# Query-major score tiles by TensorE transposes in one of eight half-steps of an attention backward pass

## The chip, the cores and the metric

The kernel runs on one core of a Trainium2 chip. The metric is the time of one execution on the device in microseconds (us). The engines are TensorE (PE; its weight loads are shown as PEld), VectorE (DVE), ScalarE (ACT), GpSimd (POOL) and SyncE (SP), which issues most of the transfers; 16 DMA engines carry them.

## What is computed

Forward and gradients of a gated sum of an attention block and a state-space convolution, sequence 2048, width 576, 32 heads of 18. The change touches only the attention:

```python
scores = jnp.einsum("bhqd,bhkd->bhqk", q, k) * (Dh ** -0.5)
p = _softmax(scores, axis=-1)
o = jnp.einsum("bhqk,bhkd->bhqd", p, v)
...
_out, _vjp = jax.vjp(_f, A_x, A_wqkv, A_wo, B_A_re, B_A_im, B_B_re, B_B_im, B_C_re, B_C_im, B_log_dt, B_Dskip, gate_w)
```

The backward pass needs the unnormalised probabilities `exp(score)` in both orientations: key-major (keys on the partitions, queries along the free axis) for the output and for the score gradient, and query-major (queries on the partitions) for the gradient of V. One is the transpose of the other.

## The kernel before

Projections come first, then the attention, then the state-space part and the last products. The attention's order on all engines is written out by hand: instructions stand on each engine in the order in which the loop issues them.

The 32 heads go in 8 groups of four, each head on 32 partitions, and the queries in 4 blocks of 512. One pair of group and block is a unit; there are 32 units. A unit takes 32 half-steps, so that the loop over `G` (L998) runs through 1024 of them, and some more at the end. A half-step does two things side by side, for two different units: the forward side for half-step `G`, and the backward side for `G2 = G - OFF`, with `OFF = 39`.

In each half-step PE issues, in this order:

- P1 (L1020-1022): two matmuls of 32 contraction rows for two heads, key-major scores of 128 keys by 512 queries, into a pair of PSUM banks (`s_pair`, tag `S`, two such pairs in rotation). ACT turns them into `PT` by one exponential of 128x1024 (L1095). There are 41 `PT` tiles in rotation, one made in each half-step.
- a burst of work that goes by slot, where slot is `(G2 + 1) % 8`: the two halves of the gradients of V (slots 0 and 1), Q (2 and 3) and K (5 and 6), or transposes that VectorE copies out (4 and 7). What a burst leaves in PSUM is evacuated by VectorE in slots 1, 3, 4, 6 and 7, but not in slots 0, 2 and 5.
- P3 (L1062-1064): two matmuls for two heads, query-major scores, into the next `S` pair. ACT turns them into `eb` by an exponential of 128x1024 (L1100). The V gradient reads `eb` in slots 0 and 1.
- P2 (L1069-1070): two matmuls for the other two heads, one PSUM bank each (tag `dP`, two banks in rotation). VectorE multiplies each by a half of `PT` into `ds` (L1105).
- accO (L1081): in slots 1, 2, 5 and 6 four more matmuls, the forward output.

The `ds` tiles are transposed by DMA (L1113), and the K gradient reads the result, `dsT`, in slots 5 and 6.

After PE's list is issued, VectorE gets first the evacuation of the burst, and then the multiplications of this half-step. ACT has two exponentials in a half-step: `PT`, then `eb`. Every eight half-steps repeat; below they are called a period. There are 128 of them.

In the profile P1 is the row `ps_P<-QaT_g,KaT_g`, P3 the row `ps_P<-KaT_g,QaT_g`, P2 the row `ps_P<-dOaT,VaT_g`, and all have the helper's line L30. Transposes of a `ds` tile are the row `turn_p` (L843), and their copy is L848.

Of the kernel before, what the change touches and what calls it, by code (L numbers as in the profile page):

```python
# [10 lines left out]
ACT = mybir.ActivationFunctionType  # L11
BF = mybir.dt.bfloat16
# [5 lines left out]
P = 128  # L18


def build(tc, aps, dbg_aps=None, stages=("s1", "attn", "post", "s4", "final")):
    nc = tc.nc
# [6 lines left out]
    def mm(out, lhsT, rhs, start=True, stop=True, **kw):  # L29
        return nc.tensor.matmul(out, lhsT=lhsT, rhs=rhs, start=start, stop=stop, **kw)  # L30
# [31 lines left out]
    with ExitStack() as gctx:  # L62
# [3 lines left out]
        ident_bf = const.tile([P, P], BF, name="ident_bf")  # L66
# [49 lines left out]
        with ExitStack() as ctx:  # L116
# [37 lines left out]
            rows = [QKV_d[ROW0[k_]:ROW0[k_] + H * WID[k_], :].rearrange("(h w) s -> h w s", w=WID[k_]) for k_ in "QKV"]  # L154
# [50 lines left out]
            for m, (h0, hn) in enumerate(hts):  # L205
                fn = hn * DH
                for which in (1, 0, 2):
# [3 lines left out]
                    for tb in range(NBK):  # L211
                        ps = psA.tile([P, TB, P], F32, tag="proj", bufs=4, name="ps_proj")
# [485 lines left out]
        if "attn" in stages:  # L698
            KB = 512
            NQ = S // KB  # L700
            TPQ = KB // P
            DA = HP
            NFILL = {"V": 1, "Q": 0, "K": 0}
            with ExitStack() as ctx:
# [9 lines left out]
                def pt_tile():  # L714

                    x = (ptn[0] - (PTN - 41)) % 41
                    ptn[0] += 1
                    return pts["a" if x < 17 else "bcd"[(x - 17) // 8]][1].tile([P, 2, KB], BF, tag="PT", name="PT")

                PTN = NG * NQ * NT * 2  # L720
                apsp = ctx.enter_context(tc.tile_pool(name="aps", reuse_waits="tile", bufs=1, space=bass.MemoryType.PSUM))
# [105 lines left out]
                def row(ps, l, r, j):  # L827
                    r0 = HP * j
                    mm(ps, lhsT=l[r0:r0 + DA], rhs=r[r0:r0 + DA], tile_position=(r0, 0))

                def s_pair(kind):
                    return apsp.tile([P, 2, KB], F32, tag="S", bufs=2, name="ps_" + kind)

                def by_pe(p):

                    return {NPF: 0, NPF + 1: 1}.get(p, 2)
# [161 lines left out]
                for G in range(NTOT + OFF + 24):  # L998
# [4 lines left out]
                    if G < NTOT:  # L1003
                        u, s = divmod(G, NST)
                        g, b = units[u]
# [7 lines left out]
                    if 0 <= G2 < NTOT:  # L1013
                        u2, s2 = divmod(G2, NST)
                        r2 = (units[u2][0], units[u2][1], s2)
                    rows = []
                    if r1:
                        g, b, i, j0 = r1
                        T = grp_t[g]
                        ps = s_pair("P1")  # L1020
# [12 lines left out]
                    elif 0 <= m_ < NTOT // 8:  # L1033
                        u_, kq = divmod(m_, NQ)
                        g, b = units[u_]
# [12 lines left out]
                        else:  # L1048
                            p = 2 * kq + (slot == 4)
# [5 lines left out]
                    if r2:  # L1055
                        g, b, s2 = r2
                        T = grp_t[g]
                        U = UN[(g, b)]
                        par_ = (s2 + OFF) % 2
                        jo = 2 * par_  # L1060
                        kq, ii = s2 // 8, (s2 % 8) // 2
                        ps = s_pair("P3")  # L1062
                        for x in range(2):
                            row(ps[:, x, :], T["QaT", b][:, ii * P:(ii + 1) * P], T["KaT", kq], jo + x)
                        rows.append(("P3", g, b, (kq, ii), jo, ps))
                        i2 = s2 // 2
                        for x in range(2):
                            j2 = 2 * (1 - par_) + x
                            ps = apsp.tile([P, KB], F32, tag="dP", bufs=2, name="ps_P2")  # L1069
                            row(ps, T["VaT", i2 // TPQ][:, (i2 % TPQ) * P:(i2 % TPQ + 1) * P], U["dOaT"].rearrange("p t q -> p (t q)"), j2)  # L1070
                            rows.append(("P2", g, b, i2, j2, ps))
                    tail = []
                    if G % 8 in (0, 3, 4, 7) and G >= 3:
                        i_ = (G - 3) // 8 * 4 + {3: 0, 4: 1, 7: 2, 0: 3}[G % 8]
                        u_, i_ = divmod(i_, NT)
                        if 0 <= u_ < NU:
                            g, b = units[u_]
# [13 lines left out]
                    for (kind, g, b, i, j, ps) in rows:  # L1091
                        U = UN[(g, b)]
                        if kind == "P1":
                            U["PT"][i, j // 2] = pt_tile()
                            nc.scalar.activation(U["PT"][i, j // 2], ps, ACT.Exp)  # L1095
                        elif kind == "P3":
                            e = work.tile([P, 2, KB], BF, tag="eb", bufs=8, name="eb")
                            for x in range(2):
                                U["eb"][(i[0], i[1], j + x)] = e[:, x, :]
                            nc.scalar.activation(e, ps, ACT.Exp)  # L1100
                        else:
                            if i not in U["ds"]:
                                U["ds"][i] = work.tile([P, 4, KB], BF, tag="ds", bufs=5, name="ds")
                                U["dsn", i] = 0
                            nc.vector.tensor_tensor(U["ds"][i][:, j, :], ps, U["PT"][i, j // 2][:, j % 2, :], op=A.mult)  # L1105
                            U["dsn", i] += 1
                            nj = 3 if by_pe(i // 2) >= 2 - i % 2 else 4
                            if U["dsn", i] == nj:
                                p = i // 2
                                assert j == nj - 1  # L1110
                                if i % 2 == 0:
                                    U["dsT", p] = work.tile([P, 2, 4 * TPQ, P], BF, tag="dsT", bufs=3, name="dsT")
                                nc.sync.dma_start_transpose(out=U["dsT", p][:, i % 2, 0:nj * TPQ, :],  # L1113
                                                            in_=U["ds"][i][:, 0:nj, :].rearrange("p j q -> p (j q)"))
# [125 lines left out]
        if "final" in stages and "s4" in stages:  # L1240
# [14 lines left out]
            with ExitStack() as ctx:  # L1255
# [18 lines left out]
                with ExitStack() as actx:  # L1274
# [10 lines left out]
                    for q, r_ in enumerate((0, 4, 12)):  # L1285
                        n_ = 2 if r_ == 12 else 1
# [89 lines left out]
                    row = pf.tile([1, D], F32, name="dlrow")  # L1376
# [19 lines left out]
                for t in range(NT):  # L1396
# [15 lines left out]
                    ps = pps.tile([P, 2, 512], F32, tag="ps2b", name="ps_a")  # L1412
# [12 lines left out]
                    ps = pps.tile([P, 2, 512], F32, tag="ps2b", name="ps_dx")  # L1425
# [17 lines left out]
                for c, (f0, fsz) in enumerate(dch):  # L1443
                    ob = work.tile([P, D], BF, tag="dwo_bf", bufs=3, name="dwo_bf")
                    for u, (e0, esz) in enumerate(HALF):
                        ps = pps.tile([P, 512], F32, tag="one", name="ps_dwo")
# [14 lines left out]
def kernel(  # L1461
    tc,
    A_x, A_wqkv, A_wo, B_u, B_A_re, B_A_im, B_B_re, B_B_im, B_C_re, B_C_im, B_log_dt, B_Dskip, gate_w, grad_out,
    out_0, out_1, out_2, out_3, out_4, out_5, out_6, out_7, out_8, out_9, out_10, out_11, out_12,
):
    aps = dict(A_x=A_x, A_wqkv=A_wqkv, A_wo=A_wo, B_u=B_u, B_A_re=B_A_re, B_A_im=B_A_im, B_B_re=B_B_re, B_B_im=B_B_im,
               B_C_re=B_C_re, B_C_im=B_C_im, B_log_dt=B_log_dt, B_Dskip=B_Dskip, gate_w=gate_w, grad_out=grad_out,
               out_0=out_0, out_1=out_1, out_2=out_2, out_3=out_3, out_4=out_4, out_5=out_5, out_6=out_6, out_7=out_7,
               out_8=out_8, out_9=out_9, out_10=out_10, out_11=out_11, out_12=out_12)
    build(tc, aps)  # L1470
# [30 lines left out]
```

The softmax here doesn't subtract the row's maximum and nothing guards it: scores larger than these inputs give would overflow.

## Time and profile before

| | us |
|---|---|
| timed runs | 2879.93 (median), 2881.84, 2875.08 |
| span of the profiled execution | 2881.9 |
| first `PT` exponential to the last `eb` exponential | 205.1 to 2180.0 |
| ACT busy in the whole span | 2374.4 |
| DVE busy in the whole span | 2361.3 |
| PE busy in the whole span | 2469.8 |

No time beside the span is recorded for the profiled execution itself; its span lies 2.0 us above the median of the timed runs. "Busy" is the union of an engine's instructions, where PE's are pipelined and their ends modelled. In the page's groups and in the timeline a row gives the start or the time in sum, the mean of one instruction, its engine, line and operation, its output and inputs, their shapes and, with x, how many there are. Neighbouring instructions overlap, so that the distance between two starts is shorter than what one of them takes.

### The profile page before, as it was taken

To read this page: it belongs to the slowest core of one execution; us is meant where nothing else is said; L and a number is where in the kernel's file an instruction comes from. 1 tells how busy PE (TensorE), PEld (TensorE's weight loads), DVE (VectorE), ACT (ScalarE), POOL (GpSimd) and SP (SyncE) were. 2 spreads that over 40 slices of the span, in tenths; PEclk is the share of its full clock that TensorE was granted. 3 is DMA by queue.
4 is the path that set the end of the run, shared out by engine and by line. 5 is a ranking of instruction groups with operands and counts; after the bars stand their busy time and mean duration, and the time that the engine had idled before them with its cause. 6 is when DMAs were issued, how large, how long until landed. Compare 5 with 4: busy or idle time off the path is not lost.

```text
span 2881.9 us, 69539 instructions
## 1 busy us (share of the span) xinstructions
PE 2469.8 (86%) x27132; PEld 1188.0 (41%) x27132; DVE 2361.3 (82%) x4143; ACT 2374.4 (82%) x2792; POOL 1609.6 (56%) x2657
## 2 busy tenths in 40 slices
PE   4778898898888889888999989898986889888699
PEld 2332333333233233233333323333324788788467
DVE  4444999898898899889999989999975899999854
ACT  2449999999899999999999999999964777877121
POOL 1037888887788888888878878888511000000010
PEclk7876999999899999999999999999966888888799
DMA  8864889999999999998998998899798888885895
GB/s 223 162 169 87 154 160 174 159 161 161 162 160 159 175 161 159 167 166 152 168 174 153 163 168 159 156 172 165 139 163 206 238 220 219 232 212 156 249 227 131
DMA packets 1293343, 499.99 MB, mean 173 GB/s; under 512 B 1187774, under 2 KB 1263136, under 8 KB 1283796
## 3 DMA queue, kind: packets, MB, share of 16 engines
q1 hardware_dynamic: 1260388, 434.38, 78.6%
q0 software_dynamic: 20624, 53.26, 7.6%
q10 hardware_dynamic: 12000, 7.90, 1.0%
q8 instruction: 212, 3.47, 0.5%
q14 instruction: 119, 0.97, 0.1%
HBM read 144.48 MB, written 99.69 MB: 85 GB/s over the span
## 4 chain that ended last, share of the span: by engine, by line
ACT 35%; PE 25%; DVE 24%; DMA 7%; issue 6%; SPq 2%; POOL 0%; ACTq 0%; DVEq 0%; POOLq 0%
ACT eb L1100 21%; ACT PT L1095 13%; PE ps_P L30 7%; DVE ds L1105 7%; DVE tz L559 3%; DMA dsT<-ds 3%; PE accV L30 2%; DVE HG L563 2%; DVE tz L562 2%; PE turn_p L843 2%; PE ps_dx L30 2%; PE ps_dwq L30 2%; PE accK L30 2%; PE accO L30 1%; DVE pq L629 1%
## 5 line engine op out<-in xcount | busy, mean ns | idle before, releaser
L1105 DVE TENSOR_TENSOR ds<-ps_P,PT 128x512 bf16<-128x512 f32 x2048 | 1312.6, 683 | 137.7 <-PE ps_P L30 89.1
L1100 ACT ACTIVATE eb<-ps_P 128x1024 bf16<-128x1024 f32 x1024 | 1097.4, 1072 | 54.6 <-PE ps_P L30 54.2
L1095 ACT ACTIVATE PT<-ps_P 128x1024 bf16<-128x1024 f32 x1024 | 1100.7, 1077 | 13.9 <-PE ps_P L30 12.8
L30 PE MATMUL ps_P<-dOaT,VaT_g 32*128 32x512 bf16 x2048 | 584.1, 392 | 31.0 <-DVE ds L1105 15.0
L358 POOL TENSOR_TENSOR et<-eG,eT 128x448 f32<-128x448 f32 x576 | 542.1, 961 | 10.7
L30 PE MATMUL ps_P<-QaT_g,KaT_g 32*128 32x512 bf16 x2048 | 411.4, 395 | 137.0 <-ACT PT L1095 122.8
L30 PE MATMUL ps_P<-KaT_g,QaT_g 32*128 32x512 bf16 x2048 | 410.2, 393 | 2.0 <-ACT eb L1100 0.9
L30 PEld LDWEIGHTS <-KaT_g 32*128 32x128 bf16 x2048 | 147.8, 91 | 474.6 <-issue 459.8
L358 POOL TENSOR_TENSOR Eo<-et,et 128x448 bf16<-128x448 f32 x288 | 327.1, 1136 | 20.7
L665 POOL TENSOR_TENSOR SS<-m 128x96 f32<-128x96 f32 x18 | 9.8, 545 | 464.9 <-ACT m L663 464.9
L30 PEld LDWEIGHTS <-QaT_g 32*128 32x128 bf16 x2048 | 116.2, 91 | 290.7 <-issue 268.4
L30 PE MATMUL accO<-PT,Vtok_g 128*32 128x512 bf16 x2048 | 213.3, 403 | 0.0
L30 PE MATMUL accV<-eb,dOa 128*32 128x512 bf16 x2048 | 188.0, 400 | 27.9 <-ACT eb L1100 27.4
L30 PE MATMUL accK<-dsT,Qtok_g 128*32 128x256 bf16 x4096 | 164.7, 282 | 31.0 <-DMA dsT<-ds 28.9
L30 PE MATMUL accQ<-ds,Ktok_g 128*32 128x512 bf16 x2048 | 161.3, 393 | 2.1 <-DVE dvacc L897 2.0
L30 PEld LDWEIGHTS <-Vtok_g 128*32 128x32 bf16 x2048 | 53.7, 93 | 227.9 <-issue 227.0
L521 ACT COPY E1e<-etp 128x1024 bf16<-128x1024 bf16 x136 | 128.2, 1039 | 18.9 <-PE etp L520 18.7
L848 DVE COPY dsT<-turn_p 128x1024 bf16<-128x1024 bf16 (+1 forms) x216 | 139.3, 645 | 5.0 <-PE turn_p L843 5.0
L843 PE MATMUL turn_p<-ident_bf,ds 128*128 128x128 bf16 x1664 | 135.8, 225 | 2.1 <-DVE dkacc L934 0.9
L30 PEld LDWEIGHTS <-E1n 128*128 128x128 bf16 x2304 | 96.5, 108 | 87.1 <-issue 86.7
L30 PEld LDWEIGHTS <-Qtok_g 128*32 128x32 bf16 x4096 | 88.9, 97 | 95.8 <-issue 62.1
L30 PE MATMUL yp<-Rw,E1n 128*128 128x30 bf16 x1152 | 67.5, 232 | 64.4 <-DVE Rw L584 50.7
(249 smaller groups left out, 3746.6 us busy)
## 6 DMA issues: line engine op xcount, KB each, us to landing
E_d<-Eo POOLq DMA_DIRECT2D x144, 256.0 KB, 3.8
E1n<-E_d SPq DMA_DIRECT2D x36, 1024.0 KB
xs<-xb_d SPq DMA_DIRECT2D x18, 1024.0 KB
T0w<-Kp_d SPq DMA_DIRECT2D x18, 1024.0 KB
Md_d<-mst SPq DMA_DIRECT2D x36, 288.0 KB
dsT<-ds SPq DMA_TRANSPOSE x512
dqkv_d<-dtk POOLq DMA_DIRECT2D x96, 72.0 KB, 4.2
QKV_d<-stg SPq DMA_DIRECT2D x12, 504.0 KB
```

The source lines that it names most:

```text
L30: return nc.tensor.matmul(out, lhsT=lhsT, rhs=rhs, start=start, stop=stop, **kw)
L358: nc.gpsimd.tensor_tensor(out, a, b, op=op)
L521: copy(E_[:, 4 * q:4 * q + 4], pt_)
L559: nc.vector.tensor_tensor(tz, HG[:, :, k - 1, :].unsqueeze(1).to_broadcast([P, 2, 4, CB]), ZZ, op=A.mult)
L562: nc.vector.tensor_tensor(t0v, t0v, UVk[:, :, :, k, :], op=A.add)
L563: nc.vector.tensor_tensor(HG[:, :, k, :].rearrange("p (r s) c -> p r s c", s=2), t0v, t1v[:, ::-1], op=A.add)
L629: nc.vector.tensor_tensor(o.rearrange("p a b n c -> p a b (n c)"), a_.rearrange("p b n c -> p b (n c)").unsqueeze(1).to_broadcast([P, 2, 2 ...
L843: nc.tensor.transpose(pt_[:, x, qb, :], t_[:, qb * P:(qb + 1) * P], ident_bf)
L848: (nc.scalar.copy if NTOT <= now[0] < NTOT + OFF else nc.vector.tensor_copy)(o_(), pt_[:, x:x + n])
L1095: nc.scalar.activation(U["PT"][i, j // 2], ps, ACT.Exp)
L1100: nc.scalar.activation(e, ps, ACT.Exp)
L1105: nc.vector.tensor_tensor(U["ds"][i][:, j, :], ps, U["PT"][i, j // 2][:, j % 2, :], op=A.mult)
```

## The change

In slot 2 (`s2 % 8 == 1`) the P3 pair isn't computed. The same numbers are taken from the four `PT` tiles of the block: eight TensorE transposes of 128x128 (two heads, four key tiles) write one PSUM tile of 128x1024 in bf16, which is one bank. It comes from the two `dP` banks, not from the `S` pairs. VectorE copies it to `eb`, where ACT had an exponential. The other seven half-steps of the period are as before.

```diff
-                        ps = s_pair("P3")
-                        for x in range(2):
-                            row(ps[:, x, :], T["QaT", b][:, ii * P:(ii + 1) * P], T["KaT", kq], jo + x)
-                        rows.append(("P3", g, b, (kq, ii), jo, ps))
+                        if s2 % 8 == 1:
+                            ps = apsp.tile([P, 2, TPQ, P], BF, tag="dP", bufs=2, name="turn_e")
+                            for x in range(2):
+                                for n_ in range(TPQ):
+                                    nc.tensor.transpose(ps[:, x, n_, :], U["PT"][TPQ * kq + n_, jo // 2][:, x, ii * P:(ii + 1) * P], ident_bf)
+                            rows.append(("PE", g, b, (kq, ii), jo, ps))
+                        else:
+                            ps = s_pair("P3")
+                            for x in range(2):
+                                row(ps[:, x, :], T["QaT", b][:, ii * P:(ii + 1) * P], T["KaT", kq], jo + x)
+                            rows.append(("P3", g, b, (kq, ii), jo, ps))
...
-                        elif kind == "P3":
+                        elif kind in ("P3", "PE"):
                             e = work.tile([P, 2, KB], BF, tag="eb", bufs=8, name="eb")
                             for x in range(2):
                                 U["eb"][(i[0], i[1], j + x)] = e[:, x, :]
-                            nc.scalar.activation(e, ps, ACT.Exp)
+                            if kind == "P3":
+                                nc.scalar.activation(e, ps, ACT.Exp)
+                            else:
+                                nc.vector.tensor_copy(e, ps.rearrange("p x n q -> p x (n q)"))
```

On the engines this is, per period: ACT one exponential fewer; PE eight transposes in place of two matmuls; VectorE one copy more, which stands ahead of that half-step's two multiplications. GpSimd's and SyncE's lists keep their instructions and order.

## Prediction

> **What bounds the kernel now.** I read the page first, its busy line, its chain of waits and its groups:
>
> ```profile
> PE 2469.8 (86%) x27132; PEld 1188.0 (41%) x27132; DVE 2361.3 (82%) x4143; ACT 2374.4 (82%) x2792; POOL 1609.6 (56%) x2657
> ...
> ACT 35%; PE 25%; DVE 24%; DMA 7%; issue 6%; SPq 2%; POOL 0%; ACTq 0%; DVEq 0%; POOLq 0%
> ...
> L1100 ACT ACTIVATE eb<-ps_P 128x1024 bf16<-128x1024 f32 x1024 | 1097.4, 1072 | 54.6 <-PE ps_P L30 54.2
> ```
>
> ACT leads the chain, but PE and DVE have a quarter each: no engine is far from the bound. The change takes 128 of the 1024 `eb` exponentials away. Next the busy times in a stretch of the attention (its columns are PE, PEld, DVE, ACT, POOL, then granted clock, DMA share and GB/s):
>
> ```profile
> 1000.00:1400.00 400.00, 355.45 (x3846) 124.31 (x3845) 356.24 (x589) 393.69 (x428) 331.03 (x542) 0.99 0.93 162
> ```
>
> ACT is busy 98%, PE and DVE 89% each, DMA 93%. Whether an exponential less is worth anything is decided in the half-step where it is taken, slot 2, so I read one period in the timeline. ACT around slot 2 (`PT` of slot 1, `eb` of slot 1, `PT` and `eb` of slot 2, `PT` of slot 3):
>
> ```profile
> 1050.08 1.07 ACT L1095 ACTIVATE PT<-ps_P 128x1024 bf16<-128x1024 f32 x1
> 1051.11 1.02 ACT L1100 ACTIVATE eb<-ps_P 128x1024 bf16<-128x1024 f32 x1
> 1052.03 1.02 ACT L1095 ACTIVATE PT<-ps_P 128x1024 bf16<-128x1024 f32 x1
> 1052.93 1.03 ACT L1100 ACTIVATE eb<-ps_P 128x1024 bf16<-128x1024 f32 x1
> 1053.84 1.04 ACT L1095 ACTIVATE PT<-ps_P 128x1024 bf16<-128x1024 f32 x1
> ```
>
> An exponential takes 1.02 to 1.08 us, but the next starts 0.90 us after it where ACT is fed in time (1052.03, 1052.93, 1053.84). So 0.90 us is what one of them occupies. The `PT` of slot 7 starts at 1046.34 and the next one at 1061.06 in this timeline, so a period is 14.72 us: 16 times 0.90 and 0.3 us in which ACT waits.
>
> PE in slot 2 (P1, first half of Q, P3, P2, accO, and the P1 of slot 3):
>
> ```profile
> 1051.28 0.39 PE L30 MATMUL ps_P<-QaT_g,KaT_g 32*128 32x512 bf16 x2
> 1051.60 0.62 PE L30 MATMUL accQ<-ds,Ktok_g 128*32 128x512 bf16 x8
> 1052.18 0.39 PE L30 MATMUL ps_P<-KaT_g,QaT_g 32*128 32x512 bf16 x2
> 1052.19 0.85 PE L30 MATMUL ps_P<-dOaT,VaT_g 32*128 32x512 bf16 x2
> 1052.98 0.40 PE L30 MATMUL accO<-PT,Vtok_g 128*32 128x512 bf16 x4
> 1053.31 0.39 PE L30 MATMUL ps_P<-QaT_g,KaT_g 32*128 32x512 bf16 x2
> ```
>
> Three things are to be seen. P3 and P2 start together: they run side by side on different rows of the array, so P3 costs PE nothing here. The P2 pair takes 0.85 and not 0.39: its second matmul starts at 1052.65, when VectorE frees its `dP` bank. And no idle time stands before the last P1: PE doesn't wait for ACT there, PE's own list is what is late. A matmul pair needs about 0.46 until ACT can start on it (P3 of slots 0 and 1 start at 1048.73 and 1050.62, their exponentials at 1049.16 and 1051.11, thus 0.43 and 0.49). P1 of slot 3 could feed ACT at 1053.31 + 0.46 = 1053.77, and ACT takes it at 1053.84. **PE is only 0.07 us ahead of ACT at the place where ACT is to be relieved.**
>
> **The change, part by part.** The new operations have rows of the same shape in the transposes of `ds` and their copy in slot 7:
>
> ```profile
> 1046.03 0.62 PE L843 MATMUL turn_p<-ident_bf,ds 128*128 128x128 bf16 x8
> 1046.62 0.39 PE L30 MATMUL ps_P<-KaT_g,QaT_g 32*128 32x512 bf16 x2
> ```
>
> ```profile
> 1046.73 0.68 DVE L848 COPY dsT<-turn_p 128x1024 bf16<-128x1024 bf16 x1
> ...
> 1051.34 2.67 DVE L1105 TENSOR_TENSOR ds<-ps_P,PT 128x512 bf16<-128x512 f32 x4
> ```
>
> Eight transposes hold PE for 0.59 (1046.03 to 1046.62); the copy starts 0.70 after their start, and takes 0.68.
>
> *Removed, ACT:* 128 exponentials at 0.90 us, 116 us if ACT alone set the pace. By the 0.07 above, the place can give back at most 0.07 x 128 = 9 us as long as PE's list is no shorter.
>
> *Removed, PE:* the P3 pair, at nothing, because P2 covers it; without that cover it would be worth 0.32 (P1 at 1051.28 to Q at 1051.60).
>
> *Added, PE:* eight transposes, 0.59. Their bank is the one of the first multiplication of slot 1, which starts at 1051.34 and ends at 1052.02, ahead of the end of Q at 1052.18: no wait.
>
> *Added, a wait:* there are two `dP` banks and now three tiles in this half-step. The transposes take the first bank, P2's first matmul the second, and P2's second matmul has to wait until VectorE has copied the first out. Step by step, with the times of this period: transposes 1052.18 to 1052.77; P2's first matmul 1052.77 (its bank is free at about 1052.6); the copy starts at 1052.18 + 0.70 = 1052.88, and VectorE is free then (second multiplication of slot 1 over by 1052.68); the copy ends at 1053.56; P2's second matmul starts about 0.06 later, at 1053.62 (that much passes in slot 4 of another period, where a multiplication ends at 1026.93 and P2 starts at 1026.99). Behind it on PE stand accO and P1 of slot 3, and ACT waits for the latter. They keep their distances, 0.33 each: accO 1053.95, P1 1054.28, ACT's `PT` 1054.28 + 0.46 = 1054.74.
>
> *Sum per period:* 1054.74 against 1053.84 is 0.90 us later, even though ACT has one exponential less. Does the rest of the period catch up? Slot 3: Q's second half 1054.60 to 1055.17, P3 then, which feeds ACT at 1055.63; ACT is ready at 1054.74 + 0.90 = 1055.64. From here ACT goes on at 0.90 as before, and the waits of slots 0 and 1 hang on ACT itself. So nothing is caught up. 128 x 0.90 = 115 us.
>
> *Moved, VectorE:* 0.60 us of issue time per period. Its second multiplication of slot 2 now waits for P2, starts near 1054.1 and ends near 1054.78 instead of 1054.01, 0.77 late where ACT is 0.90 late; in slots 3 to 1 VectorE is thus no nearer to the bound, and I cost the copy's own time at nothing. If that cover were gone, it would be 0.60 x 128 = 77 us.
>
> *Moved, the `S` pairs and `PT`:* P1 of slot 3 gets a pair that ACT left long before, which can't help while PE is late. The oldest `PT` tile is now read one half-step longer, and its place is written again by ACT in slot 3; the transposes stand ahead of that P1 on PE, so it costs nothing.
>
> *DMA:* no transfer is added. The 32 `oT` copies, one per unit, start between 238.3 and 2097.1: 1858.8 / 31 / 4 = 14.99 us per period, 0.27 above the undisturbed 14.72, which is 33 us over 124 periods. Most of it is K's wait for `dsT`:
>
> ```profile
> PE accK L30 <- DMA dsT<-ds: 20.1, 12, 5.2
> ```
>
> A further 14.1 us of waits for the same transfers stand at its weight loads. With 6% more time per period the DMA share falls from 0.93 to about 0.88, and part of these waits goes: between 0 and 33 us, and I take half, 16.
>
> *Total:* 2881.9 + 115 - 16 = 2981 for an execution like the profiled one. This lies 2.0 above the median of the runs, so 2979. For the unknown ends: without any wait for the copy, P2's pair goes at 1052.77, P1 at 1053.43 and ACT at 1053.89, 0.05 x 128 = 6 us; with the copy one VectorE operation late (0.60) it is 1.50 x 128 = 192 us. I take the value of the two rows, because the shapes are the same and VectorE is free.
>
> The page "TensorE: Matmul & The Clock Gate" of the Trainium skill (section on the PE-mode transpose) speaks against the change more strongly than the trace: it has about 275 ns for one transpose inside a kernel, and says that the transposes don't count as activity for the clock. Eight at 275 ns are 2.2 us by estimate, 1.61 more than the row's 0.59, or 206 us on top. The trace has eight in 0.59 us, so I go by the row; its clock in the stretch above, 0.99 with 340 such transposes, doesn't decide the second point.
>
> **The rivals.** *Faster:* ACT's 0.90 us comes through in slot 2, 2881.9 - 116 = 2766, median 2764. For it speaks ACT's 98%. It decides if P1 of slot 3 starts by 1052.93 - 0.46 = 1052.47, and breaks even if it starts by 1053.38; PE's list puts Q, transposes, P2 and accO before it, and Q alone ends at 1052.18. 5%.
>
> *No wait:* the copy is out before PE needs the bank, +6 us, and the DMA waits shrink by as much or more: 2865 to 2888. Against it: copying can't begin before the last transpose, and the first P2 stands right behind that. 4%.
>
> *The clock falls:* PE idles about 0.85 us more in slot 2. Between 2110 and 2130, where P1 and accO are missing, the granted clock is 0.50. Were it so throughout, PE's part from P1 to P1, 0.32 + 0.58 + 0.59 + 0.33 + 0.33 = 2.15, doubles: +2.15 x 128 = 275 us, near 3255; where only one period in five falls, 55 us, near 3035. Against it: P1 and accO, missing there, are still in every period, and today's DMA waits of up to 5.2 us leave the clock at 0.99 over the stretch. 10%, most of it near the low end.
>
> *Main forecast:* 81%, its own range 2940 to 3010 from the DMA term (0 to 33) and 0.15 us either way in the chain (19 us).
>
> **The numbers.** About 0.2% (6 us) is what can be told from no change. Faster 5%, same 4% (the no-wait case is put here, and a little of it could be faster), slower 91%. The range 2925 to 3035 leaves out the faster case, the no-wait case and the deep end of the clock case.
>
> **What would show it.** In slot 2 after: an idle of about 0.8 us on PE before the second P2, released by the new copy; `PT` of slot 3 about 2.7 us after `PT` of slot 2 instead of 1.81; a period of about 15.6 us; ACT busy near 87% in the attention with its idle time before `PT`, released by PE. The forecast is wrong if the copy ends before P2 is issued, if ACT stays at 98%, or if the clock drops outside DMA waits.

## The result, and the profile after

The changed kernel takes 2961.25 us (median of 4 runs, 2960.17 to 2965.21), the kernel before 2878.54 us on the same chip. The ratio is 1.0276 with a 95% interval of 1.0253 to 1.0300: slower by 2.8%, 83 us. The profiled execution has a span of 2958.9 us, 77.0 us more than the one before. The forecast was 2979 us, 2925 to 3035. Of e2_actcopy's four runs below, two (3194.25 and 3210.19 us) were slower at a lower granted clock (0.83 and 0.82 against 0.86 and 0.87), and its time and ratio are those of the other two.

The page of the changed kernel, its busy line, its chain of waits and the group of the `PT` exponentials (L1102 now; `eb` is L1108, `ds` L1115, the new transposes L1066 and their copy L1110):

```profile
PE 2531.0 (86%) x27900; PEld 1236.4 (42%) x27900; DVE 2436.5 (82%) x4271; ACT 2261.4 (76%) x2664; POOL 1610.5 (54%) x2657
...
PE 31%; ACT 31%; DVE 23%; issue 7%; DMA 5%; SPq 2%; POOL 0%; ACTq 0%; DVEq 0%; POOLq 0%
...
L1102 ACT ACTIVATE PT<-ps_P 128x1024 bf16<-128x1024 f32 x1024 | 1077.2, 1054 | 222.9 <-PE ps_P L30 222.2
```

ACT has 113 us less work, and its idle time ahead of the `PT` exponentials, released by PE, has become 222.2 us. Before, that group's idle was 13.9 us. PE has gone from 25% to 31% of the chain. The same stretch of the attention as before (PE, PEld, DVE, ACT, POOL, clock, DMA share, GB/s):

```profile
1000.00:1400.00 400.00, 356.87 (x3783) 129.56 (x3780) 351.30 (x579) 349.92 (x378) 318.69 (x533) 0.97 0.90 155
```

ACT is busy 87% there where it was 98%, the DMA share fell from 0.93 to 0.90. Slot 2 in the timeline, first PE:

```profile
1049.11 0.39 PE L30 MATMUL ps_P<-QaT_g,KaT_g 32*128 32x512 bf16 x2
1049.42 0.61 PE L30 MATMUL accQ<-ds,Ktok_g 128*32 128x512 bf16 x8
1049.97 0.62 PE L1066 MATMUL turn_e<-ident_bf,PT 128*128 128x128 bf16 x8
1050.53 0.38 PE L30 MATMUL ps_P<-dOaT,VaT_g 32*128 32x512 bf16 x1
1051.44 0.37 PE L30 MATMUL ps_P<-dOaT,VaT_g 32*128 32x512 bf16 x1 [0.53 <-DVE eb L1110]
1051.74 0.40 PE L30 MATMUL accO<-PT,Vtok_g 128*32 128x512 bf16 x4
1052.08 0.39 PE L30 MATMUL ps_P<-QaT_g,KaT_g 32*128 32x512 bf16 x2
```

The pair of P2 is torn apart. Its first matmul follows the transposes at once, the second starts 0.91 us later, 0.53 of it idle, and the releaser is the new copy. From P1 of slot 2 to P1 of slot 3 it takes 2.97 us where it took 2.03. VectorE beside it:

```profile
1049.17 1.28 DVE L1115 TENSOR_TENSOR ds<-ps_P,PT 128x512 bf16<-128x512 f32 x2
1050.70 0.69 DVE L1110 COPY eb<-turn_e 128x1024 bf16<-128x1024 bf16 x1 [0.25 <-PE turn_e L1066]
1051.31 1.28 DVE L1115 TENSOR_TENSOR ds<-ps_P,PT 128x512 bf16<-128x512 f32 x2
```

The copy starts 0.73 us after the first transpose, ends at 1051.39, and P2 goes 0.05 us later. And ACT:

```profile
1049.80 1.02 ACT L1102 ACTIVATE PT<-ps_P 128x1024 bf16<-128x1024 f32 x1
1052.51 1.02 ACT L1102 ACTIVATE PT<-ps_P 128x1024 bf16<-128x1024 f32 x1 [1.69 <-PE ps_P L30]
```

From `PT` of slot 2 to `PT` of slot 3 it is 2.71 us; before, with an exponential in between, it was 1.81. Over the attention, the waits say how often:

```profile
ACT PT L1102 <- PE ps_P L30: 209.1, 124, 2.4
...
PE ps_P L30 <- DVE eb L1110: 66.3, 124, 0.9
```

209.1 / 124 is 1.69 us on average, and there are 124 such waits in the 128 periods.

To separate what happens in every period from what happens now and then, I use the distance between neighbouring `oT` copies (L781), one per unit of four periods. In both kernels 16 of the 31 units lie within 0.1 us of the commonest length: 58.92 us before, 62.22 after. This commonest length is called the undisturbed unit below. What the other units take beyond it is the excess (waits for transfers and low clock are in it): 32.3 us before, 13.9 after, over 31 units. So the attention's stretch of 83.9 us is 31 x 3.30 = 102.3 us more of undisturbed units and 18.4 us less of excess. The other 7 us of the span's difference, the opposite way, lie ahead of the first copy (1.4) and behind the last (5.5). The latter part ranges from 777.7 to 789.1 us over the profiles of this study, so I read nothing into it.

The sizes fit single periods too. From `PT` of slot 2 to the next `PT` of slot 2, a period most often takes 14.73 us before and 15.55 after.

### The profile page after: what moved, and what is told of

Read it like the earlier page. It is cut to its first block, busy times and chain, and to the rows that moved or that the text cites. A ratio compares the mean times of both kernels' runs of the same rounds, so it can differ in the third digit from the quotient of the medians.

```text
span 2958.9 us, 70571 instructions
## 1 busy us (share of the span) xinstructions
PE 2531.0 (86%) x27900; PEld 1236.4 (42%) x27900; DVE 2436.5 (82%) x4271; ACT 2261.4 (76%) x2664; POOL 1610.5 (54%) x2657
## 4 chain that ended last, share of the span: by engine, by line
PE 31%; ACT 31%; DVE 23%; issue 7%; DMA 5%; SPq 2%; POOL 0%; ACTq 0%; DVEq 0%; POOLq 0%
ACT eb L1108 18%; ACT PT L1102 12%; PE ps_P L30 9%; DVE ds L1115 5%; PE accQ L30 4%; PE accO L30 4%; DVE tz L559 3%; DVE eb L1110 3%; PE turn_e L1066 2%; DVE tz L562 2%; DVE HG L563 2%; PE accV L30 2%; PE ps_dx L30 2%; PE ps_dwq L30 2%; DVE pq L629 1%
## 5 line engine op out<-in xcount | busy, mean ns | idle before, releaser
L1115 DVE TENSOR_TENSOR ds<-ps_P,PT 128x512 bf16<-128x512 f32 x2048 | 1311.7, 683 | 93.9 <-PE ps_P L30 88.8
L1102 ACT ACTIVATE PT<-ps_P 128x1024 bf16<-128x1024 f32 x1024 | 1077.2, 1054 | 222.9 <-PE ps_P L30 222.2
L1108 ACT ACTIVATE eb<-ps_P 128x1024 bf16<-128x1024 f32 x896 | 944.1, 1054 | 41.9 <-PE ps_P L30 40.8
L30 PE MATMUL ps_P<-dOaT,VaT_g 32*128 32x512 bf16 x2048 | 592.4, 390 | 93.6 <-DVE eb L1110 68.1
L30 PE MATMUL ps_P<-KaT_g,QaT_g 32*128 32x512 bf16 x1792 | 358.4, 393 | 1.1 <-ACT eb L1108 0.6
L30 PEld LDWEIGHTS <-QaT_g 32*128 32x128 bf16 x1792 | 100.2, 91 | 230.9 <-issue 209.2
L795 POOL TENSOR_TENSOR dOa<-dO_b,rl 128x288 bf16<-128x288 bf16 x32 | 21.5, 673 | 250.8 <-DVE rl L790 250.8
```

## The experiments

All ratios are to the kernel before on the same chip (2884 to 2888 us in the runs e1 to e9). The undisturbed unit and the excess are worked out from the `oT` rows of each trace as above, and "half clock" is the time at a granted clock of 0.50 between the first and the last of these rows. The undisturbed unit of e2_actcopy rests on only 5 of its 31 units, the others on 9 to 27. Each diff is against the kernel that the expectation below it starts from.

| kernel | us | ratio (95%) | undisturbed unit | excess | half clock |
|---|---|---|---|---|---|
| before | 2878.54 | 1 | 58.92 | 32.3 | 84 |
| changed | 2961.25 | 1.0276 (1.0253 to 1.0300) | 62.22 | 13.9 | 89 |
| e1_pair | 2931.17 | 1.0150 (1.0127 to 1.0173) | 59.97 | 51.1 | 165 |
| e2_actcopy | 3121.96 | 1.0810 (1.0770 to 1.0851) | 63.50 | 140.5 | 570 |
| e3_onemm | 3007.66 | 1.0426 (1.0396 to 1.0455) | 61.28 | 98.6 | 425 |
| e4_accO | 2946.95 | 1.0207 (1.0175 to 1.0238) | 60.21 | 60.5 | 210 |
| e5_pair_act | 2920.10 | 1.0108 (1.0080 to 1.0136) | 59.42 | 61.7 | 199 |
| e6_act_dummy | 2995.28 | 1.0385 (1.0355 to 1.0415) | 63.48 | 9.3 | 48 |
| e7_onemm_dummy | 2955.11 | 1.0235 (1.0208 to 1.0262) | 61.88 | 9.7 | 40 |
| e8_dummy | 2961.48 | 1.0262 (1.0237 to 1.0286) | 62.21 | 13.5 | 50 |
| e9_onemm_turns | 2948.01 | 1.0230 (1.0194 to 1.0266) | 61.93 | 8.0 | 40 |

### e1_pair: the transposes in another bank

```diff
-ps = apsp.tile([P, 2, TPQ, P], BF, tag="dP", bufs=2, name="turn_e")
+ps = s_pair("turn_e").bitcast(BF)[:, 0, :].rearrange("p (x n q) -> p x n q", x=2, q=P)
```

> The transposes write half of an S pair instead of a dP bank; transposes, copy and ACT's saving stay. Theory A (the loss is the wait of P2's second matmul for VectorE's copy through the two dP banks): the pair of P2 goes together right behind the transposes, the 0.53 us idle of PE is gone and P1 of slot 3 comes 0.88 us earlier than in the changed kernel, so PT of slot 2 to PT of slot 3 falls from 2.71 to about 1.83 us (1.81 before). 2961 - 128 x 0.88 = 2848, plus the DMA waits that come back at the faster pace (0 to 20): 2850 to 2890, about the kernel before. Theory B (what costs is the extra work on PE and VectorE, 0.56 and 0.60 us per period, whatever the bank): stays at 2940 to 2961.

In the place itself theory A held: `PT` of slot 2 to `PT` of slot 3 is 1.81 us (median over 120 periods), and the undisturbed unit lost 2.25 us, 0.56 per period. So taking the wait at the bank away gains 0.56 x 128 = 72 us, net of what comes up in its place. ACT has an exponential less there and gains nothing by it, because it waits for PE:

```profile
1179.65 1.02 ACT L1102 ACTIVATE PT<-ps_P 128x1024 bf16<-128x1024 f32 x1 [0.79 <-PE ps_P L30]
```

But the time, 2931, lies between what A and B gave. One part of that is the excess, which grew from 13.9 to 51.1 us. The other part is in the unit, which is still 1.05 us longer than before the change: three of its four periods take 14.83 us (14.73 before), the first takes 15.49. In the three, a wait has come up three half-steps later. VectorE in the trace of e1_pair, from the copy on:

```profile
1178.74 0.69 DVE L1110 COPY eb<-ps_turn_e 128x1024 bf16<-128x1024 bf16 x1 [0.25 <-PE ps_turn_e L1066]
1179.35 1.28 DVE L1115 TENSOR_TENSOR ds<-ps_P,PT 128x512 bf16<-128x512 f32 x2
1180.55 0.68 DVE L915 SCALAR_TENSOR_TENSOR gb<-accQ,dqa 128x512 bf16<-128x512 f32 x1
1181.14 1.28 DVE L1115 TENSOR_TENSOR ds<-ps_P,PT 128x512 bf16<-128x512 f32 x2
1182.34 0.68 DVE L848 COPY dsT<-turn_p 128x1024 bf16<-128x1024 bf16 x1
1182.94 2.47 DVE L1115 TENSOR_TENSOR ds<-ps_P,PT 128x512 bf16<-128x512 f32 x4
```

Each row starts where the one before leaves off (0.60 us per operation): VectorE has no gap from slot 2 to slot 5. PE then waits for it, and ACT for PE:

```profile
1184.27 0.37 PE L30 MATMUL ps_P<-dOaT,VaT_g 32*128 32x512 bf16 x1 [0.23 <-DVE ds L1115]
1184.57 0.40 PE L30 MATMUL accO<-PT,Vtok_g 128*32 128x512 bf16 x4
1184.90 0.39 PE L30 MATMUL ps_P<-QaT_g,KaT_g 32*128 32x512 bf16 x2
```

```profile
1184.20 1.06 ACT L1108 ACTIVATE eb<-ps_P 128x1024 bf16<-128x1024 f32 x1
1185.33 1.02 ACT L1102 ACTIVATE PT<-ps_P 128x1024 bf16<-128x1024 f32 x1
```

`PT` of slot 6 starts 1.13 us after the `eb` ahead of it, not 0.90. In the changed kernel this can't be seen, because the wait in slot 2 gives VectorE time. In the first period of a unit VectorE also copies `oT`, ahead of slot 3's evacuation `dqa`, and in slot 4 PE's transposes of `oT` (`accF`) wait 0.61 us for `dqa` each time:

```profile
PE accF L785 <- DVE dqa L915: 19.2, 31, 0.8
```

Before the change there are 2 such waits, 1.0 us together.

### e5_pair_act: the same, copied by ACT

```diff
-nc.vector.tensor_copy(e, ps.rearrange("p x n q -> p x (n q)"))
+nc.scalar.copy(e, ps.rearrange("p x n q -> p x (n q)"))
```

> As e1_pair, but the copy of the transposed tile is made by ACT. PE's list is the same; ACT has its 16 operations per period again, VectorE is rid of 0.60 us. Theory A (what e1_pair still lost, 0.26 us per period, is VectorE's copy, which runs VectorE without a gap from slot 2 to slot 5): the late PT of slot 6 (1.13 us after its forerunner in e1_pair) comes back to 0.90 to 0.92, the undisturbed unit falls from 59.97 us to between 58.9 and 59.3, and the time is that of the kernel before plus 0 to 30 us (2885 to 2915 on this chip). Rival (the transposes on PE): the unit stays at 59.9 us and the time at 2930.

The wait of slot 6 is gone (0.90 us), and the undisturbed unit fell by 0.55 us, 0.14 per period on average: this is VectorE's share. It fell to 59.42 and not to 59.3, and the time to 2920, not to 2915, since the excess grew to 61.7 us. What is left of the unit, 0.50 us over the kernel before, lies in one period of the four: three take 14.73 us, as before the change, so that the transposes on PE cost nothing there. The first takes 15.23, and PE's wait for `dqa` is still in it, 0.43 us each time:

```profile
PE accF L785 <- DVE dqa L915: 13.8, 31, 0.8
```

VectorE comes late to `dqa`, since in slot 2 it stands idle for 0.60 us until P2, which has the transposes ahead of it. This is read from the trace; I did not take the transposes away in this kernel to show it.

### e4_accO: a shorter list in slot 2

```diff
-if G % 8 in (0, 3, 4, 7) and G >= 3:
-    i_ = (G - 3) // 8 * 4 + {3: 0, 4: 1, 7: 2, 0: 3}[G % 8]
+if G % 8 in (0, 1, 3, 4, 7) and G >= 3:
+    i_ = (G - 3) // 8 * 4 + {3: 0, 4: 1, 7: 2, 0: 3, 1: 3}[G % 8]
...
-if 0 <= u_ < NU:
+if 0 <= u_ < NU and not (G % 8 < 2 and (G % 8 == 0) != (i_ == NT - 1)):
```

> As e1_pair (transposes in half of an S pair), and the forward output's matmuls of slot 2 are issued one half-step later, in slot 3, in three of four periods. Theory A (the length of PE's list between P1 of slot 2 and P1 of slot 3 sets the pace there, and ACT has 0.9 us to gain): 0.3 us sooner in 96 periods, e1_pair minus 29 us, less what the DMA waits take: 2825 to 2870, faster than before. Rival (PE, VectorE and DMA are all full, the gain is lost in slot 3 or to dsT): within 10 us of e1_pair.

A miss for theory A, and worse than the rival had it. `PT` of slot 2 to `PT` of slot 3 came down to 1.50 us (median), 0.31 less than in e1_pair, as expected; but `eb` of slot 3 to `PT` of slot 4 went from 0.92 to 1.47. What slot 2 gains, slot 3 loses. PE has accO there as well now, and P2 goes later: in one period its second matmul starts 0.90 us after P3, where it was 0.59 in e1_pair, with VectorE's multiplication as the releaser, and P1 of slot 4 starts 1.53 us after P3, where it was 0.63. ACT waits 0.45 us for it.

### e2_actcopy and e3_onemm: the copy on ACT, and no transposes

```diff
-nc.vector.tensor_copy(e, ps.rearrange("p x n q -> p x (n q)"))
+nc.scalar.copy(e, ps.rearrange("p x n q -> p x (n q)"))
```

> As the changed kernel, but the copy of the transposed tile is made by ACT instead of VectorE, through the same dP bank. Theory A (wait for the copy): ACT's copy of this shape takes 1.02 us where VectorE's takes 0.69, and ACT is free at about the time at which the transposes end, so P2's second matmul and PT of slot 3 come 0.33 us later: 2961 + 128 x 0.33 = 3003 (2985 to 3015). Theory B (VectorE's load): VectorE is rid of 0.60 us per period, so the time falls below 2961, at most by 77 us.

```diff
-for x in range(2):
-    for n_ in range(TPQ):
-        nc.tensor.transpose(ps[:, x, n_, :], U["PT"][TPQ * kq + n_, jo // 2][:, x, ii * P:(ii + 1) * P], ident_bf)
+ps = apsp.tile([P, KB], F32, tag="dP", bufs=2, name="turn_e")
+row(ps, T["QaT", b][:, ii * P:(ii + 1) * P], T["KaT", kq], jo)
...
-U["eb"][(i[0], i[1], j + x)] = e[:, x, :]
+U["eb"][(i[0], i[1], j + x)] = e[:, 0 if kind == "PE" else x, :]
...
-nc.vector.tensor_copy(e, ps.rearrange("p x n q -> p x (n q)"))
+nc.vector.tensor_copy(e[:, 0, :], ps)
```

> The eight transposes are left out: one score matmul of 32 rows by 512 columns fills the dP bank in their place, VectorE copies its 512 float32 columns (0.69 us, as long as the copy of the transposes), and both heads' tiles are that one copy without an exponential, so the V gradient is another one. The bank and the wait for the copy stay. Theory A: the copy can start as soon as VectorE is through with slot 1, about 0.25 us earlier than in the changed kernel, and only this is gained: 2961 - 128 x 0.25 = 2929 (2915 to 2940), still slower than before. Rival (the transposes' own 0.56 us on PE is the loss): 2961 - 128 x 0.56 = 2889 or less.

In the undisturbed unit both came out at theory A's size: 0.32 us per period more with the copy on ACT (0.33 expected), 0.24 less without the transposes (0.25 expected). In e3_onemm the copy is the releaser of P2's second matmul, as expected. In e2_actcopy it isn't:

```profile
1053.57 0.37 PE L30 MATMUL ps_P<-dOaT,VaT_g 32*128 32x512 bf16 x1 [0.85 <-DVE ds L1115]
```

P2's second matmul starts 0.05 us after the end of VectorE's multiplication of the first, and 0.02 us before the recorded end of ACT's copy, so it doesn't wait for the copy. That the sizes agree is luck. What e2_actcopy does show is that a longer wait of this matmul, 0.85 us for 0.53, lengthens the period by as much.

The times were 3122 and 3008, some 120 and 80 us above what theory A gave. What neither theory had is in the clock. The stretch from 1000 to 1400 of e2_actcopy and of e3_onemm; the third number from the end is the clock:

```profile
1000.00:1400.00 400.00, 354.93 (x3650) 126.76 (x3650) 327.90 (x536) 364.47 (x391) 306.25 (x503) 0.93 0.89 151
```

```profile
1000.00:1400.00 400.00, 362.87 (x3436) 118.49 (x3432) 336.49 (x552) 338.31 (x361) 303.06 (x498) 0.85 0.86 149
```

Between the first and the last `oT` copy PE ran at half clock for 570 and 425 us, against 89 in the changed kernel.

### e6 to e8: dummy matmuls in the wait

```diff
 for x in range(2):
     j2 = 2 * (1 - par_) + x
+    if x == 1 and s2 % 8 == 1:
+        fill(s_pair("warm")[:, 0, :], 2)
```

(In e8_dummy one in place of two.)

> As e2_actcopy, with two dummy matmuls of 128x512 (into a pair of banks that nobody reads) in PE's wait for the copy in slot 2. Theory A (e2_actcopy's time beyond 3003 us is PE's clock, which fell because PE stood still for longer: 570 us at half clock in its trace): the clock stays up, the undisturbed unit stays at 63.5 us, the mean unit falls from 68.0 to about 64, time 3000 to 3035. Rival (ACT or the transfers make the long units): stays above 3100.

> As e3_onemm (transposes left out, one matmul without an exponential for two heads), with the same two dummy matmuls in PE's wait. Theory A (without the transposes PE's activity fell below what keeps the clock; the wait alone was 0.24 us shorter, as expected): clock up, unit 61.3 us, mean unit 61.5 to 62, time 2930 to 2960. Rival: stays at 3000.

> As the changed kernel, with one dummy matmul of 128x512 in the 0.53 us in which PE waits for the copy. Theory A (the wait sets the loss; the clock costs the changed kernel at most the 14 us by which its units exceed 62.22): undisturbed unit 62.22 as before, time 0 to 12 us under the changed kernel, ratio to the kernel before 1.024 to 1.028. Rival (the clock is a large part of the loss): 30 us or more under the changed kernel, ratio 1.017 or less.

The clock was the cause: with work that nobody reads in the wait, e2_actcopy lost 127 us and e3_onemm 53 us. The same stretch of e6_act_dummy:

```profile
1000.00:1400.00 400.00, 363.09 (x3805) 132.53 (x3797) 337.16 (x555) 371.43 (x402) 310.55 (x506) 1.00 0.93 155
```

The undisturbed unit of e6 is that of e2 (63.48 and 63.50), so the wait itself stayed, and 2995, a little under the 3000 to 3035 expected, is close to the 3003 that the wait alone gives. In e7 the two dummies were a little longer than the wait: 2.62 us from `PT` to `PT`, against 2.47 in e3_onemm. In the changed kernel itself (e8) the dummy halves the time at half clock and changes neither unit nor excess; the time is the same within its interval. So the changed kernel's loss isn't the clock. A small part of its excess is: ten of its units are 0.45 to 0.56 us longer than the commonest, each with 3.4 us at half clock and hardly a wait for transfers in it, 5 us together. In e8 no unit is like that, but waits for transfers make up for it. One thing is left open: the fillers of e6 to e9 also take an `S` pair out of turn, and no run takes the pair without filling it.

### e9_onemm_turns: transposes in place of the dummies

```diff
     if x == 1 and s2 % 8 == 1:
-        fill(s_pair("warm")[:, 0, :], 2)
+        w_ = s_pair("warm").bitcast(BF)[:, 0, :].rearrange("p (a q) -> p a q", q=P)
+        for n_ in range(8):
+            nc.tensor.transpose(w_[:, n_, :], U["PT"][TPQ * kq + n_ // 2, 0][:, n_ % 2, 0:P], ident_bf)
```

> As e7_onemm_dummy, but what fills PE's wait in slot 2 are eight transposes of 128x128 (into a pair of banks that nobody reads) in place of the two dummy matmuls. If transposes count as activity for PE's clock: little time at half clock (under 100 us in the attention, as the dummies' 40), unit 61.3 to 62, time 2935 to 2965. If they don't (the page's statement): about 425 us at half clock and 3000 us, as e3_onemm.

In this wait transposes keep the clock up as well as the dummies did: 40 us at half clock, as with the dummies, and 2948 us. PE in its slot 2, and its stretch from 1000 to 1400:

```profile
1055.76 0.37 PE L30 MATMUL ps_P<-dOaT,VaT_g 32*128 32x512 bf16 x1
1056.07 0.62 PE L1077 MATMUL ps_warm<-ident_bf,PT 128*128 128x128 bf16 x8
1056.62 0.38 PE L30 MATMUL ps_P<-dOaT,VaT_g 32*128 32x512 bf16 x1
```

```profile
1000.00:1400.00 400.00, 365.39 (x3866) 132.56 (x3865) 358.99 (x588) 356.28 (x386) 324.67 (x529) 1.00 0.91 157
```

The eight fill the time between the two P2 matmuls, and the clock of the stretch is 1.00, where it was 0.85 in e3_onemm.

## Why the prediction was right, point by point

**The place.** "PE is only 0.07 us ahead of ACT at the place where ACT is to be relieved" was the step that ruled a gain out, and it held: no kernel here that takes the exponential away is faster than before, not even e1_pair (1.0150), where the wait at the bank is gone and `PT` of slot 3 comes 1.81 us after `PT` of slot 2 as before. In e4_accO slot 2 became 0.31 us shorter, and the rest of the period took that back.

**The wait.** The chain was right link by link: transposes 0.56 (0.59 forecast), copy 0.73 after their start (0.70), P2 0.05 after the copy (0.06), 2.71 us from `PT` to `PT` (2.71). That the last agrees to the hundredth is partly luck: from P1 to P1 it was 2.97 (3.00), from P1 to `PT` in slot 3 0.43 (0.46), and `PT` of slot 2 came 0.69 after its P1 (0.75). The idle time on PE was 0.53 and not the 0.8 named as a sign; the forecast had counted from the start of P2's first matmul, which itself takes 0.38.

e1_pair shows that the wait is what costs: 0.72 of the 0.82 us in three of four periods, where VectorE's copy has the other 0.10 (e5_pair_act is back at 14.73) and the transposes nothing. In the first period of a unit only 0.07 comes back, and 0.50 stays even with the copy on ACT. On average that is 0.56, 0.14 for VectorE's copy, and 0.13 that was read from the trace and not shown by a run.

**The size.** The sum per period was 0.90 and came out as 3.30 / 4 = 0.825. The step that was off is "So nothing is caught up". Slots 0 and 1 gave back 0.11 us: from `PT` to `eb` it is 0.96 and 0.97 there, where it was 1.02 and 1.03. Slot 3 took 0.04. For slot 0 a reading fits: in a run of exponentials started 0.90 apart their recorded durations grow, to 1.15 us at `PT` of slot 7 before but only to 1.10 after, for the gap in slot 2 starts the growth afresh; P1 of slot 0 waits for the end of that exponential. No run was made to test this. For slot 1 it doesn't fit: the recorded durations there are as before, and what is shorter is the time from P3 to `eb`, 0.43 us where it was 0.49; why is open. Both slots together are 0.07 x 128 = 10 us of the 18 by which the forecast was too high. Most of the rest, 7 us, lies outside the stretch between the `oT` copies.

**The transfers.** 16 us were to come back, and the excess fell by 18.4. PE's waits for `dsT`, at K's matmuls and their weight loads, fell from 34.2 to 8.1 us in the attention.

**VectorE's cover.** Its 0.60 us were costed at nothing under the wait, and at 77 us with the cover gone. With the cover gone (e1_pair) they cost 0.14 per period, 18 us: 0.10 in three periods of a unit and 0.26 in the first. The rest fits into VectorE's gaps.

**The rivals.** The no-wait case was priced at 2865 to 2888, "+6 us": e1_pair is that case and has 2931. That price left out VectorE without its cover, the first period of each unit, and the excess, which grew from 32 to 51 us instead of shrinking.

The clock rival came only in small (0.97 in the stretch), but it did come, and with it one of the forecast's signs of being wrong, a clock that drops outside DMA waits. After the start of the attention the changed kernel has 16 records of half clock, and 13 of them have no wait of PE for a transfer of over 0.5 us in the 10 us ahead; before the change each of the 7 has one. It cost about 5 us (see e8_dummy), which the forecast's sum doesn't have. The rival was also nearer than its 10% sound: 0.32 us more of wait per period, or 8 transposes fewer, brought it on.

The page "TensorE: Matmul & The Clock Gate" of the Trainium skill (section on the PE-mode transpose), which the forecast weighed, has about 275 ns for one transpose inside a kernel. One is recorded at 0.22 us here, but eight in a row start 0.06 us apart and take 0.56 together, so that eight times the page's figure was not their price. The page also says that transposes don't count as busy time for the clock in the way that matmuls do; in e9_onemm_turns eight of them in the wait did for the clock what two matmuls did in e7_onemm_dummy (40 us at half clock in both, 425 without).

## What to carry to other kernels

Relieving the busiest engine gave nothing here, because the other engines' lists at that very place had no time to spare; compare the start of the next matmul that feeds it with when it would be wanted, there and not on average. A third tile in a rotation of two banks ties a later user to an earlier one's evacuation; count the tiles per step before reusing a tag, and look in the trace for the releaser, because a time that agrees doesn't name it (e2_actcopy). After a change, look at the distance of a row that comes once per loop: its commonest value shows the schedule, what lies above it shows transfers and clock, and they must be explained apart. Take the shortest loop for it: the period showed what the unit of four periods averages away.

## What was not expected of the hardware

PE's clock stands near an edge in this loop. In e2_actcopy PE's idle time in slot 2 is 0.85 us in a period of 15.87, where it is 0.53 in 15.55 in the changed kernel. No idle time of PE between the first and the last `oT` copy is longer than 0.86 us, and yet the time at half clock rose from 89 to 570 us and the excess from 13.9 to 140.5; with two matmuls of no use in that wait (e6_act_dummy) they are 48 and 9.3. The granted clock in these records is 0.50 or 1.0 and nothing in between.

How long PE stands still is not the whole of it. e1_pair, e4_accO and e5_pair_act have no such wait, and PE is busier in them (370.72 us of the stretch from 1000 to 1400 in e5_pair_act, 355.45 before the change), but they have 165 to 210 us at half clock against 84 before. What the clock goes by stays open. In the wait of slot 2, 128x128 transposes did for it what matmuls did.
